# An attention and gated-MLP kernel rewritten around PSUM bank pairs and an order from a table

## The chip, the cores and the metric

The program runs on one core of one Trainium2 chip. A core has a matrix engine (TensorE, PE in the profile), a vector engine (VectorE, DVE), a scalar engine (ScalarE, ACT), GpSimd (POOL) and SyncE (SP), which here only issues transfers. Each engine works through its own instructions strictly in the order in which they stand, and waits for other engines on semaphores. Matmuls write to PSUM, a memory of eight banks of 512 float32 values for each of 128 partitions; ACT and DVE read PSUM, POOL can't. The metric is the time of one execution on the device, in microseconds (us); lower is better.

## The reference

The computation has two stages over 8 batches of 576 tokens. The first is a linear attention with 8 heads of width 64, the second a gated MLP over the 512 values that the heads give for each token.

```python
def phi(x):                                   # for q and for k
    proj = x @ w_phi                          # 64 -> 128 features
    proj = proj - max(abs(proj), over the features)
    return concat([exp(proj), exp(-proj)])    # 256 features
kv  = phi(k).T @ v                            # for each batch and head: 256 x 64
z   = sum of phi(k) over the tokens
x   = (phi(q) @ kv) / (phi(q) @ z + 1e-6)     # heads side by side: 576 x 512
h   = relu(x @ w_in)                          # 512 -> 1024
u, w = h[:, :512], h[:, 512:]
w   = (w - mean(w)) / sqrt(var(w) + 1e-6)     # over the 512 columns
w   = w_spatial @ w + b_spatial               # over the 576 tokens
out = (u * w) @ w_out                         # 512 -> 512
```

## The kernel before

Each batch's 576 tokens are four blocks of 128 ("main") and a tail of 64; the tails of two batches are joined to one block of 128. A unit of the first stage is one pair of heads of one batch (all four blocks), or the joined tail of two batches (all eight heads): 32 and 4 units. For a unit, q and k are brought to feature-major form, by PE transposes for the first batches and by transfers that transpose for the later ones; `by_token` (L229) then projects half a unit, four token-by-head blocks, into one PSUM bank with two matmuls of 256 columns, whose moving operand `wphi2` holds w_phi twice on a diagonal, for the two heads of a pair. For keys (`a_keys`, L236) DVE takes the maximum of the absolute values of that bank (L244) and ACT then takes exp(x) and exp(-x) of it (L247): each of the three instructions is 512 wide. The maximum of the keys is applied to v instead (`a_scale`, L264, multiplied on POOL at L272). Queries are projected twice. Once by token for the maximum (`a_queries`, L258); the maximum is split in a high and a low bfloat16 part (`mhl`), turned on PE (L293), and then subtracted inside the second, feature-major projection (`a_qfeat`, L296) by matmuls with the selection matrix `sel` (L308, 128 columns each). ACT takes both exponentials of it, again 512 wide (L321). `a_kv` (L326, matmuls L334 and L336) sums keys against values, `a_num` (L347, L354) multiplies query features with that sum, and `norm` (L341) divides on DVE (L344, L345).

The second stage, for one batch at a time, is `b_v` (L403, ReLU on ACT, statistics on DVE), `b_ln` (normalization on POOL, L420, with a root of four instructions, L413 to L416), `b_u` (L456), `b_s` (L477, gate on DVE, L480) and `b_o` (L500, copied by ACT, L502). It is PE work above all: matmuls of 512 columns.

Every PSUM tile of the kernel before is one bank, taken in turn from a pool of eight (`psum`, L57), and the framework places the semaphores. It also orders two engines that only read the same bank: the exponentials L247 wait for the maximum L244 of the same bank, though they don't use it.

The order of the work is made by loops. `step(i)` (L580) emits the parts of the units that are due (`ORDER`, L560, with lags of some units), and after each part `fill` (L568) emits tasks of the second stage from a queue, by a credit that counts PE's time. Loads are issued by POOL and SP from `io` (L622), some units ahead.

Of the kernel before, what the change touches and what calls it, by code (L numbers as in the profile page):

```python
# [12 lines left out]
AX = mybir.AxisListType  # L13


@with_exitstack
def kernel(
# [14 lines left out]

    nc = tc.nc

# [5 lines left out]
    P = 128  # L40
    KC = DM // P
    NP = H // 2
# [3 lines left out]
    G = B // 2  # L46
    POS = [0, 2, 1, 3]
    DA = D + 2

    cpool = ctx.enter_context(tc.tile_pool(name="const", bufs=1))  # L50
    ld = ctx.enter_context(tc.tile_pool(name="loads", bufs=2))
    a1 = ctx.enter_context(tc.tile_pool(name="stage_a", bufs=2))
    feat = ctx.enter_context(tc.tile_pool(name="feat", bufs=2))
    small = ctx.enter_context(tc.tile_pool(name="small", bufs=3))
    s2 = ctx.enter_context(tc.tile_pool(name="stage_b", bufs=2))

    psum = ctx.enter_context(tc.tile_pool(name="psum", bufs=8, space=bass.MemoryType.PSUM))  # L57


    def pin(start):  # L60
        return lambda *a, **kw: tc.keep_in_program_order(start(*a, **kw))

    def main_ap(t, b, h0=0, n=H):
        return bass.AP(tensor=t.tensor, offset=t.offset + (b * H + h0) * S * D,
                       ap=[[NB * D, P], [S * D, n], [1, NB * D]])
# [5 lines left out]
    st = {}  # L71
    gs = {}

    XB = 2

    def alloc(b):
        st[b] = dict(
            q=ld.tile([P, H, NB * D], BF16, tag="q_bf", name="q_bf", bufs=2),
            k=ld.tile([P, H, NB * D], BF16, tag="k_bf", name="k_bf", bufs=2),
            v=ld.tile([P, H * NB, D], FP32, tag="v_f", name="v_f"),  # L80
        )

    def alloc_tail(g):
        gs[g] = dict(
            q=ld.tile([P, H, D], BF16, tag="q_tl", name="q_tl", bufs=1),
            k=ld.tile([P, H, D], BF16, tag="k_tl", name="k_tl", bufs=1),
            v=ld.tile([P, H, D], FP32, tag="v_tl", name="v_tl", bufs=1),
        )

    def load(x, b, h0=0, n=H):  # L90
        if b not in st:
            alloc(b)
        pin(nc.gpsimd.dma_start)(out=st[b][x][:, h0:h0 + n], in_=main_ap(q if x == "q" else k, b, h0, n))

    def load_v(b, eng):
        pin(eng.dma_start)(out=st[b]["v"].rearrange("p (h c) d -> p h (c d)", h=H), in_=main_ap(v, b))

    def load_tail(x, g):
        if g not in gs:
            alloc_tail(g)  # L100
        t, eng = dict(q=(q, nc.gpsimd), k=(k, nc.gpsimd), v=(v, nc.sync))[x]
        for i in range(2):
            pin(eng.dma_start)(out=gs[g][x][i * TL:(i + 1) * TL], in_=tail_ap(t, 2 * g + i))

    def cross(b):
        d = st[b]
        for x in ("k", "q"):
            d[x + "T"] = ld.tile([P, 2 * H, P], BF16, tag=x + "T_b", name=x + "T_b", bufs=2)
            pin(nc.sync.dma_start_transpose)(out=d[x + "T"], in_=d[x].rearrange("p h x -> p (h x)"))


    wphi_f = cpool.tile([P, F], FP32)
    for i in range(2):
        nc.scalar.dma_start(out=wphi_f[i * D:(i + 1) * D, :], in_=w_phi)
    alloc(0)
    first = {}
    for x, t in (("k", k), ("q", q)):
        first[x] = s2.tile([P, 2, NB * D], FP32, tag="ob", name="first", bufs=4)
        pin(nc.sync.dma_start)(out=first[x], in_=main_ap(t, 0, 0, 2))
    ident = cpool.tile([P, P], BF16)  # L120
    make_identity(nc, ident)
    zero = cpool.tile([P, 1], BF16)
    pin(nc.vector.memset)(zero, 0.0)
    wphi2 = cpool.tile([P, 2 * F], BF16)
    pin(nc.vector.memset)(wphi2, 0.0)
    neghalf = cpool.tile([P, NB + 1], FP32)
    pin(nc.vector.memset)(neghalf, -0.5)

    w_spT = cpool.tile([P, NB + 2, S], BF16)
    pin(nc.vector.memset)(w_spT[:, NB:NB + 2, :], 0.0)  # L130

    NM = 3
    mhl, mT = [], []
    for i in range(NM):
        for tiles, name in ((mhl, "mhl"), (mT, "mT")):
            t = cpool.tile([P, P], BF16, name=f"{name}{i}")
            pin(nc.vector.memset)(t, 0.0)
            tiles.append(t)

    sel1 = cpool.tile([P, H], BF16)  # L140
    sel = cpool.tile([P, H, F], BF16)
    pin(nc.vector.tensor_tensor)(out=sel1, in0=ident[:, 0:H], in1=ident[:, H:2 * H], op=ALU.add)
    pin(nc.vector.tensor_scalar)(out=sel, in0=sel1.unsqueeze(2).to_broadcast([P, H, F]), scalar1=-1.0,
                                 scalar2=None, op0=ALU.mult)
    for x in ("k", "q"):
        pin(nc.vector.tensor_copy)(out=st[0][x][:, 0:2], in_=first[x])
    vst, vnt = [], []
    for i in range(2):
        t = cpool.tile([P, 2, 2, H, DA], BF16, name=f"vst{i}")
        pin(nc.scalar.copy)(out=t.rearrange("p b s h d -> p (b s h d)"), in_=zero.to_broadcast([P, 4 * H * DA]))  # L150
        vst.append(t)
        if i == 0:
            for y in range(2):
                r = slice(y * D, (y + 1) * D)
                pin(nc.scalar.copy)(out=wphi2[r, y * F:(y + 1) * F], in_=wphi_f[r, :])
        t = cpool.tile([P, 2, HALF], BF16, name=f"vnt{i}")
        for bl, row in ((0, TL), (1, 0)):
            pin(nc.scalar.copy)(out=t[:, bl, :], in_=ident[:, row:row + 1].to_broadcast([P, HALF]))
        vnt.append(t)
    load_v(0, nc.sync)  # L160
    for x in ("k", "q", "v"):
        load_tail(x, 0)
    load("k", 0, 2, 2)
    load("q", 0, 2, 2)
    load("k", 0, 4, 4)
    load("q", 0, 4, 4)

    w_in_bf = cpool.tile([P, KC, DFF], BF16)
    w_out_bf = cpool.tile([P, KC, DM], BF16)
    wsp = s2.tile([P, NB, T0], BF16, tag="vn", name="wsp", bufs=2)  # L170
    wspr = cpool.tile([P, NB, TL], BF16)
    wspt = ld.tile([TL, S], BF16, tag="kT_b", name="wspt", bufs=2)
    bsp_row = ld.tile([P, S], FP32, tag="qT_b", name="bsp_row", bufs=2)
    nc.sync.dma_start(out=bsp_row[TL:TL + 1, :], in_=moe_b_spatial)
    nc.sync.dma_start(out=bsp_row[0:1, :], in_=moe_b_spatial)

    rows = moe_w_spatial[0:T0, :].rearrange("(p c) s -> p c s", c=NB)
    cols = moe_w_in.rearrange("(kc p) f -> p kc f", p=P)

    def load_weight(out, in_):  # L180
        pin(nc.gpsimd.dma_start)(out=out, in_=in_)

    EARLY = 5
    XX = 9
    EK = 7
    def transpose_spatial(i):

        pt = psum.tile([P, S], BF16, tag="bank", name="pt")
        if i < NB:
            sc = POS[i]  # L190
            for tp, c in enumerate(POS):
                nc.tensor.transpose(out=pt[:, tp * P:(tp + 1) * P], in_=wsp[:, c, bass.ds(sc, P, step=NB)],
                                    identity=ident)
            nc.tensor.transpose(out=pt[:, T0:S], in_=wspt[:, bass.ds(sc, P, step=NB)],
                                identity=ident[:TL, :TL])
            nc.vector.tensor_copy(out=w_spT[:, i, :], in_=pt)
            return
        for bl in range(2):
            lo = bl * TL
            for tp, c in enumerate(POS):  # L200
                nc.tensor.transpose(out=pt[lo:lo + TL, tp * P:(tp + 1) * P], in_=wspr[:, c, :], identity=ident)
            nc.tensor.transpose(out=pt[lo:lo + TL, T0:S], in_=wspt[:, T0:S], identity=ident[:TL, :TL])
            nc.vector.tensor_copy(out=w_spT[lo:lo + TL, NB + bl, :], in_=pt[lo:lo + TL, :])
        for bl, row in ((0, TL), (1, 0)):
            r = slice(row, row + 1)
            pin(nc.scalar.copy)(
                out=w_spT[r, NB + bl, 0:T0].rearrange("o (a b p) -> o a b p", a=2, b=2),
                in_=bsp_row[r, 0:T0].rearrange("o (p b a) -> o a b p", a=2, b=2))
            pin(nc.scalar.copy)(out=w_spT[r, NB + bl, T0:S], in_=bsp_row[r, T0:S])


    def a_transpose(u):
        src = st[u["b"]] if u["pair"] else gs[u["g"]]
        if "kT" in src:
            for x in ("kT", "qT"):
                u[x] = src[x][:, 4 * u["pj"]:4 * u["pj"] + 4, :] if u["pair"] else src[x]
            return
# [18 lines left out]
    def a_keys(u):  # L236
# [4 lines left out]
        for half in range(2):  # L241
# [4 lines left out]
            for s, sc in ((0, 1.0), (1, -1.0)):  # L246
                nc.scalar.activation(out=u["kf"][:, s, hs, :], in_=pk, func=AF.Exp, bias=0.0, scale=sc)  # L247
# [436 lines left out]
```

## Time and profile before

| | |
|---|---|
| time, median of 3 runs | 289.59 us (288.79 to 296.42) |
| span of the profiled execution, first to last instruction | 286.4 us |
| median less that span | 3.2 us |
| granted TensorE clock | 1.000 |
| PE busy | 261.6 us (91%), 3070 matmuls |
| ACT busy | 229.3 us (80%), 517 instructions |
| DVE busy | 201.8 us (70%), 509 instructions |
| POOL busy | 182.2 us (64%), 320 instructions |
| first matmul | 4.29 us after the span's start |

The profile is of one execution. Its own time is known by its span of 286.4 us; what lies around the span is taken as the 3.2 us by which the median exceeds it. A busy time is the union of an engine's instructions from their starts to their ends. Instructions of one engine overlap in their ends (the next starts before the last has written all), so what an instruction costs in a row of its kind is the distance from its start to the next start, and is less than its mean duration; the timeline shows both.

### The profile page before, as it was taken

The page shows a single profiled execution, that of the slowest core. Times are in us where ns is not written, and L with a number is a line of the kernel's source. Part 1 is how long each engine was busy: PE and PEld are TensorE (multiplying, and loading weights), DVE is VectorE, ACT ScalarE, POOL GpSimd, SP SyncE. Part 2 cuts the span into 40 slices and gives each one's busy share as a digit, 9 for nine tenths or more (in the row PEclk, how much of TensorE's full clock was granted, in tenths as well). Part 3 has the DMA queues.
Part 4 walks back from the last instruction along what each step waited for, and adds up shares of the span by engine and source line. Part 5 has one row for each costly group of instructions (what it writes and reads, how often), then busy time and mean ns, then how long its engine had stood idle before and what let it go on. Part 6 is the DMA issues. An engine that isn't in the chain of part 4 may idle for free.

```text
span 286.4 us, 7965 instructions
## 1 busy us (share of the span) xinstructions
PE 261.6 (91%) x3070; PEld 178.6 (62%) x3070; DVE 201.8 (70%) x509; ACT 229.3 (80%) x517; POOL 182.2 (64%) x320
## 2 busy tenths in 40 slices
PE   1378889999999999999989999999999999999983
PEld 1157776777666776767557687666667676545441
DVE  4389997977958877598696887578688864354610
ACT  4949998899799988999998679799999746566033
POOL 8159998798336899479689954835969600058200
PEclk9999999999999999999999999999999999999999
DMA  6989999976568499999955994999111003500037
GB/s 185 203 171 120 206 219 223 163 203 71 79 147 186 102 187 155 173 245 196 130 94 102 225 191 87 264 287 255 32 22 32 7 2 122 211 3 0 0 90 242
DMA packets 81706, 40.31 MB, mean 141 GB/s; under 512 B 50242, under 2 KB 77058, under 8 KB 81668
## 3 DMA queue, kind: packets, MB, share of 16 engines
q1 hardware_dynamic: 54180, 28.32, 43.0%
q0 software_dynamic: 27328, 11.41, 35.5%
q8 instruction: 24, 0.39, 0.6%
q14 instruction: 14, 0.11, 0.2%
q10 hardware_dynamic: 160, 0.07, 0.1%
HBM read 32.85 MB, written 9.44 MB: 148 GB/s over the span
## 4 chain that ended last, share of the span: by engine, by line
PE 61%; ACT 14%; DVE 11%; DMA 9%; POOL 2%; issue 2%; ACTq 0%; SPq 0%; POOLq 0%; DVEq 0%
PE pv L403 10%; PE ps L477 8%; PE po L500 7%; PE pu L456 7%; PE ps L232 5%; ACT qf L321 5%; ACT kf L247 5%; PE pv L334 4%; DMA q_tl<-in_q_dram 4%; PE pn L354 4%; DMA out_dram<-ob 3%; PE pq L308 3%; PE pq L304 3%; DVE mk L244 3%; PE ps L478 2%; DVE mq L258 2%
## 5 line engine op out<-in xcount | busy, mean ns | idle before, releaser
L247 ACT ACTIVATE kf<-ps 128x512 bf16<-128x512 f32 x144 | 77.7, 692 | 5.6 <-DVE mk L244 5.4
L272 POOL TENSOR_TENSOR vs<-v_f,em 128x512 bf16<-128x512 f32 x64 | 65.6, 1049 | 23.6 <-ACT em L267 22.6
L321 ACT ACTIVATE qf<-pq 128x512 bf16<-128x512 f32 x128 | 68.2, 675 | 8.5 <-PE pq L308 8.5
L244 DVE TENSOR_REDUCE mk<-ps 128x4 f32<-128x512 f32 x72 | 46.1, 677 | 2.5 <-PE ps L232 2.0
L258 DVE TENSOR_REDUCE mq<-ps 128x4 f32<-128x512 f32 x62 | 39.9, 681 | 4.2 <-PE ps L232 3.4
L502 ACT COPY ob<-po 128x512 f32<-128x512 f32 (+1 forms) x37 | 21.6, 610 | 19.9 <-PE po L500 16.2
L406 DVE BATCH_NORM_STATS2 stats<-vr 128x6 f32<-128x512 bf16 (+1 forms) x37 | 24.8, 687 | 15.8 <-ACT vr L405 15.7
L477 PE MATMUL ps<-w_spT,vn 128*128 128x512 bf16 x128 | 32.8, 379 | 0.0
L456 PE MATMUL pu<-xT,w_in_bf 128*128 128x512 bf16 x128 | 31.6, 379 | 0.0
L403 PE MATMUL pv<-w_in_bf,xT 128*128 128x512 bf16 x128 | 31.2, 379 | 0.0
L480 DVE TENSOR_TENSOR uT<-ps,uT 128x512 bf16<-128x512 f32 x32 | 22.0, 689 | 12.7 <-PE ps L478 11.5
L500 PE MATMUL po<-w_out_bf,uT 128*128 128x512 bf16 x128 | 30.4, 379 | 0.0
L308 PE MATMUL pq<-mT,sel 128*128 128x128 bf16 x256 | 30.0, 219 | 0.0
L308 PEld LDWEIGHTS <-sel 128*128 128x128 bf16 x256 | 25.1, 98 | 3.9
L405 ACT ACTIVATE vr<-pv 128x512 bf16<-128x512 f32 (+1 forms) x37 | 23.3, 691 | 4.0 <-PE pv L403 3.9
L354 PEld LDWEIGHTS <-qf 128*128 128x128 bf16 x512 | 20.4, 97 | 8.2 <-issue 1.7
L345 DVE TENSOR_TENSOR x<-pn,rc 128x256 bf16<-128x256 f32 x64 | 25.0, 418 | 0.5
L420 POOL TENSOR_SCALAR vn<-vr,rs 128x512 bf16<-128x512 bf16 x32 | 24.3, 773 | 0.8
L334 PE MATMUL pv<-vs,kf 128*128 128x66 bf16 x512 | 24.5, 194 | 0.2 <-ACT kf L247 0.2
L354 PE MATMUL pn<-kv,qf 128*128 128x66 bf16 x512 | 22.3, 193 | 1.3 <-ACT qf L321 1.2
L334 PEld LDWEIGHTS <-kf 128*128 128x128 bf16 x512 | 21.7, 97 | 1.8 <-issue 0.9
L304 PE MATMUL pq<-qT_b,wphi 128*128 128x256 bf16 x96 | 22.4, 273 | 0.0
(120 smaller groups left out, 530.8 us busy)
## 6 DMA issues: line engine op xcount, KB each, us to landing
v_f<-in_v_dram SPq DMA_DIRECT2D x8, 1024.0 KB, 10.7
out_dram<-ob SPq DMA_DIRECT2D x32, 256.0 KB, 3.6
k_bf<-in_k_dram POOLq DMA_DIRECT2D x7, 512.0 KB, 7.0
q_bf<-in_q_dram POOLq DMA_DIRECT2D x7, 512.0 KB, 8.7
v_tl<-in_v_dram SPq DMA_DIRECT2D x8, 128.0 KB, 7.7
w_in_bf<-in_moe_w_in_dram POOLq DMA_DIRECT2D x2, 512.0 KB, 8.7
out_dram<-ob SPq DMA_DIRECT2D x8, 128.0 KB, 2.4
k_tl<-in_k_dram POOLq DMA_DIRECT2D x8, 64.0 KB, 6.8
```

The source lines that it names most:

```text
L244: nc.vector.tensor_reduce(out=u["mk"][:, hs], in_=pk, axis=AX.X, op=ALU.max, apply_absolute_value=True)
L247: nc.scalar.activation(out=u["kf"][:, s, hs, :], in_=pk, func=AF.Exp, bias=0.0, scale=sc)
L258: nc.vector.tensor_reduce(out=mq[:, 4 * half:4 * half + 4], in_=pq, axis=AX.X, op=ALU.max, apply_absolute_value=True)
L272: nc.gpsimd.tensor_tensor(out=vs[:, s, :, 0:D], in0=st[u["b"]]["v"][:, pj * H:(pj + 1) * H, :], in1=em[:, s, :].unsqueeze(2).to_broadcast( ...
L308: nc.tensor.matmul(out=pq[:, 2 * par + x, :], lhsT=sel[:, j, :], rhs=m, start=False, stop=(x == 1))
L321: nc.scalar.activation(out=qf[:, s], in_=pq, func=AF.Exp, bias=0.0, scale=sc)
L334: nc.tensor.matmul(out=pv[:, hh, s, :], lhsT=u["kf"][:, s, 4 * hh + c, :], rhs=u["vs"][:, s, 4 * hh + c, :], start=(c == 0), stop=False)
L354: nc.tensor.matmul(out=pn[:, pos, :], lhsT=u["qf"][hh][:, s, pos, :], rhs=d["kv"][:, 2 * u["pj"] + hh, s, :], start=(s == 0), stop=(s == 1))
L403: nc.tensor.matmul(out=pv[r], lhsT=lhs(kc), rhs=w_in_bf[:, kc, HALF:DFF], start=(kc == 0), stop=(kc == KC - 1))
L456: nc.tensor.matmul(out=pu, lhsT=w_in_bf[:, kc, dc * P:(dc + 1) * P], rhs=d["xT"][:, kc, :], start=(kc == 0), stop=(kc == KC - 1))
L477: nc.tensor.matmul(out=ps, lhsT=d["vn"][:, sp, cs], rhs=w_spT[:, sp, 0:T0], start=(sp == 0), stop=False)
L500: nc.tensor.matmul(out=po[r], lhsT=lhs(dc), rhs=w_out_bf[:, dc, :], start=(dc == 0), stop=(dc == KC - 1))
```

## The change

The kernel is written anew; the computation, the engines that take most of its parts and the number of cores stay. What differs:

- **Query units.** A unit of queries is two token blocks by four heads (32 units), no longer four blocks by two heads. Key units stay a pair of heads by four blocks.
- **Half-row projections.** `wphi` holds w_phi twice, one copy in partitions 0 to 63 and one in 64 to 127. A projection contracts 64 partitions: the even head's matmul uses the upper half of the array's rows and the odd head's the lower half, each writing another bank. By token that is eight matmuls of 128 columns for a unit; feature-major it is two of 512 columns, and eight with half of `sel`.
- **Operations over bank pairs.** All of PSUM is one tile `ps` of eight banks; `pair(i, j)` is an access pattern over banks i and j, with the step j - i. The maxima, the exponentials and the division of a unit each read such a pair in one instruction of 1024 (the division 512) elements.
- **Order and places from a table.** `ORDER` is a text of 1418 words. Each names a part of the work with its indices, the numbers of the buffers or banks it takes, and the engine where there is a choice. The words are emitted from the first to the last, with no scheduler and no pools behind them. 56 of its 144 bank pairs are neighbours, 25 are six or seven banks apart.
- **Smaller moves.** 34 of the 72 ReLUs, 13 of the 36 output copies and 11 of the 32 copies of the key sums go to DVE; the root is one instruction on DVE and one on POOL, for two blocks; transposes by transfer are of half a batch; the tails of batches 0 and 1 are joined as the others are; 18 matmuls on the identity stand at the start.

```diff
-    psum = ctx.enter_context(tc.tile_pool(name="psum", bufs=8, space=bass.MemoryType.PSUM))
+    psum = ctx.enter_context(tc.tile_pool(name="ps", bufs=1, space=bass.MemoryType.PSUM))
+    ps = psum.tile([P, 8, 512], FP32, name="banks")
...
+    def bank(i):
+        return ps[:, i, :]
+
+    def pair(i, j):
+        return ps[:, bass.ds(i, 2, step=j - i), :]
...
-    def by_token(xT, half):
-        ps = psum.tile([P, 4, F], FP32, tag="bank", name="ps")
-        for x in range(2):
-            nc.tensor.matmul(out=ps[:, 2 * x:2 * x + 2, :], lhsT=xT[:, 2 * half + x, :], rhs=wphi2,
-                             start=True, stop=True)
-        return ps
+    def by_token(xT, banks):
+        for n in range(HH):
+            for y in range(2):
+                nc.tensor.matmul(out=bank(banks[y])[:, n * F:(n + 1) * F], lhsT=xT[halves[y], n, :],
+                                 rhs=wphi[halves[y], :], start=True, stop=True)
+        return pair(*banks)
+
+    def maxima(out_, pp):
+        nc.vector.tensor_reduce(out=out_, in_=pp.rearrange("p y (n f) -> p y n f", f=F), axis=AX.X, op=ALU.max,
+                                apply_absolute_value=True)
+
+    def key_exp(pp, kf, s):
+        nc.scalar.activation(out=kf[:, s].rearrange("p y n f -> p y (n f)"), in_=pp, func=AF.Exp, bias=0.0,
+                             scale=(1.0, -1.0)[s])
...
+    def features(u, xT, banks):
+        m = at["mT", u]
+        for y in range(2):
+            nc.tensor.matmul(out=bank(banks[y]).rearrange("p (n t) -> p n t", n=HH), lhsT=wphi[halves[y], :],
+                             rhs=xT[halves[y]], start=True, stop=False)
+        for n in range(HH):
+            for y in range(2):
+                nc.tensor.matmul(out=bank(banks[y])[:, n * P:(n + 1) * P], lhsT=sel[halves[y], n, :],
+                                 rhs=m[halves[y], :], start=False, stop=(n == HH - 1))
+        at["pq", u] = pair(*banks)
+
+    def query_exp(u, s):
+        nc.scalar.activation(out=at["qf", u][:, s].rearrange("p y n t -> p y (n t)"), in_=at["pq", u], func=AF.Exp,
+                             bias=0.0, scale=(1.0, -1.0)[s])
+
+    def sums(banks):
+        return pair(*banks)[:, :, 0:HH * DA].rearrange("p y (n d) -> p y n d", d=DA)
...
+    def qx(e, b, cc, hg, place=None):
+        u = (b, cc, hg)
+        if place is not None:
+            take("x", (b, cc), place)
+        nc.vector.tensor_tensor(out=at["x", (b, cc)][:, :, hg * HH:(hg + 1) * HH, :], in0=at["pn", u][:, :, :, 0:D],
+                                in1=at["rc", u].to_broadcast([P, 2, HH, D]), op=ALU.mult)
...
+    with tc.manual_schedule():
+        for word in ORDER.split():
+            word, _, e = word.partition("@")
+            name, _, places = word.partition(":")
+            name, *args = name.split(".")
+            places = [int(x) for x in places.split(",")] if places else []
+            ops[name](e, *map(int, args), *places)
```

One line of the table, as an example: keys are projected by `kp` (batch, pair of heads, two banks), their maxima are `km`, their exponentials `ke`; queries are `qp`, `qm`, `qf`, `qe`; `qn` multiplies with the key sums, `qr` and `qx` divide.

```
qr.0.0.0:1 qx.0.0.0:1 lq.2:2 qn.0.0.1:2,5 lv.1.1:1@S xq.1.1:0 ckt.1:0@P km.1.0:1 kp.1.1:4,6 lqt.1:1@S qr.0.0.1:2
qx.0.0.1 xk.2.0:2 tx.0.1:2 qe.0.1.1.0:3 km.1.1:0 qe.0.1.1.1 tx.0.0:5 ke.1.0.0:4 qn.0.1.1:1,3 vst.0.1.0@P txc.0.0:0@V
```

More of the change, by code (lines that the diff above doesn't have):

```diff
@@ L105, in cross @@
[L105 to L119, printed above, removed]
@@ L140 @@
[L140 to L159, printed above, removed]
@@ L174 @@
[L174 to L188, printed above, removed]
+    rows = [slice(0, TL), slice(TL, 2 * TL)]
@@ new lines, in zsp, with warm, lkf @@
+    @op
+    def zsp(e):
+        ENG[e].memset(w_spT[:, NB:NB + 2, :], 0.0)
+    @op
+    def warm(e, n, place):
+        for i in range(n):
+            nc.tensor.matmul(out=bank(place)[:, 0:F], lhsT=ident, rhs=ident, start=True, stop=True)
+    @op
+    def lkf(e, j, *places):
+        if j == 0:
+            take("ld", ("k", 0), places[0])
+        take("ob", ("k", j), places[-1])
+        ENG[e].dma_start(out=at["ob", ("k", j)].rearrange("p (h x) -> p h x", h=2), in_=main_ap(k, 0, 2 * j, 2))
@@ new lines, in ckt, with cqt, lvt, lin @@
+    @op
+    def ckt(e, g, place):
+        copy(e, take("tl", ("k", g), place), at["tf", ("k", g)])
+    @op
+    def cqt(e, g, place):
+        copy(e, take("tl", ("q", g), place), at["tf", ("q", g)])
+    @op
+    def lvt(e, g, place):
+        t = take("vt", g, place)
+        for i in range(2):
+            ENG[e].dma_start(out=t[rows[i]], in_=tail_ap(v, 2 * g + i))
+    @op
+    def lin(e, i):
+        cs = slice(HALF, DFF) if i == 0 else slice(0, HALF)
+        nc.gpsimd.dma_start(out=w_in[:, :, cs], in_=moe_w_in.rearrange("(kc p) f -> p kc f", p=P)[:, :, cs])
@@ new lines, in xk, with xq, turn @@
+    @op
+    def xk(e, b, h2, place):
+        cross("k", b, h2, place)
+    @op
+    def xq(e, b, h2, place):
+        cross("q", b, h2, place)
+    def turn(x, b, h2, i, place):
+        pt = bank_bf(place).rearrange("p (n t) -> p n t", t=P)
+        src = at["ld", (x, b)][:, h2 * HH:(h2 + 1) * HH]
+        for j in range(4):
+            nc.tensor.transpose(out=pt[:, j, :], in_=src[:, 2 * i + j // 2, (j % 2) * P:(j % 2 + 1) * P],
+                                identity=ident)
+        at["pT", (x, b, h2, i)] = pt[:, 0:4, :]
@@ new lines, in turn_tail, with tkt, tqt, tktc @@
+    def turn_tail(x, g, place):
+        pt = bank_bf(place).rearrange("p (n t) -> p n t", t=P)
+        for j in range(HH):
+            nc.tensor.transpose(out=pt[:, j, :], in_=at["tl", (x, g)][:, 2 * j:2 * j + 2, :], identity=ident)
+        at["pT", (x, g)] = pt[:, 0:HH, :]
+    @op
+    def tkt(e, g, place):
+        turn_tail("k", g, place)
+    @op
+    def tqt(e, g, place):
+        turn_tail("q", g, place)
+    @op
+    def tktc(e, g, place):
+        copy(e, take("tT", ("k", g), place), at["pT", ("k", g)])
@@ new lines, in qe, with qn @@
+    def qe(e, b, cc, hg, s, place=None):
+        if place is not None:
+            take("qf", (b, cc, hg), place)
+        query_exp((b, cc, hg), s)
+    @op
+    def qn(e, b, cc, hg, p0, p1):
+        u = (b, cc, hg)
+        f = at["qf", u]
+        at["pn", u] = sums((p0, p1))
+        for y in range(2):
+            for n in range(HH):
+                for s in range(2):
+                    nc.tensor.matmul(out=at["pn", u][:, y, n, :], lhsT=f[:, s, y, n, :],
+                                     rhs=at["kv", b][:, hg * HH + n, s, :], start=(s == 0), stop=(s == 1))
@@ new lines, in qnt, with qrt @@
+    @op
+    def qnt(e, g, p0, p1):
+        at["pn", g] = sums((p0, p1))
+        for y in range(2):
+            for n in range(HH):
+                for s in range(2):
+                    for bl in range(2):
+                        r = rows[bl]
+                        nc.tensor.matmul(out=at["pn", g][r, y, n, :], lhsT=at["qf", g][:, s, y, n, r],
+                                         rhs=at["kv", 2 * g + bl][:, 2 * n + y, s, :], start=(s == 0), stop=(s == 1))
+    @op
+    def qrt(e, g, place):
+        nc.vector.reciprocal(out=take("rc", g, place), in_=at["pn", g][:, :, :, D:D + 1])
@@ new lines, in um, with ur @@
+    @op
+    def um(e, b, dc, place):
+        for kc in range(KC):
+            nc.tensor.matmul(out=bank(place).rearrange("p (c t) -> p c t", c=NB),
+                             lhsT=w_in[:, kc, dc * P:(dc + 1) * P], rhs=at["xT", b][:, :, kc, :], start=(kc == 0),
+                             stop=(kc == KC - 1))
+        at["pu", (b, dc)] = bank(place)
+    @op
+    def ur(e, b, dc, place=None):
+        if place is not None:
+            take("uT", b, place)
+        relu(e, at["uT", b][:, dc, :], at["pu", (b, dc)])
@@ new lines, in om, with oc, od @@
+    @op
+    def om(e, b, c, place):
+        for dc in range(KC):
+            nc.tensor.matmul(out=bank(place), lhsT=at["uT", b][:, dc, c * P:(c + 1) * P], rhs=w_out[:, dc, :],
+                             start=(dc == 0), stop=(dc == KC - 1))
+        at["po", (b, c)] = bank(place)
+    @op
+    def oc(e, b, c, place):
+        copy(e, take("ob", (b, c), place), at["po", (b, c)])
+    @op
+    def od(e, b, c):
+        dst = bass.AP(tensor=out.tensor, offset=out.offset + (b * S + c) * DM, ap=[[NB * DM, P], [1, DM]])
+        ENG[e].dma_start(out=dst, in_=at["ob", (b, c)])
@@ L648 @@
[L648 to L653 removed]
+            for c in range(NB):
+                nc.tensor.matmul(out=pt[:, dc, :], lhsT=at["vn", 2 * g + bl][:, c, cs], rhs=w_spT[:, c, T0:S],
+                                 start=(c == 0), stop=False)
+            nc.tensor.matmul(out=pt[:, dc, :], lhsT=at["vnt", g][:, bl, cs], rhs=w_spT[:, NB + bl, T0:S],
+                             start=False, stop=True)
@@ new lines, in smt, with sgt, omt, oct @@
+        at["psp", g, bl] = pt
+    @op
+    def sgt(e, g, bl):
+        u = at["uTt", g][:, :, rows[bl]]
+        nc.vector.tensor_tensor(out=u, in0=at["psp", g, bl], in1=u, op=ALU.mult)
+    @op
+    def omt(e, g, place):
+        for dc in range(KC):
+            nc.tensor.matmul(out=bank(place), lhsT=at["uTt", g][:, dc, :], rhs=w_out[:, dc, :], start=(dc == 0),
+                             stop=(dc == KC - 1))
+        at["po", g] = bank(place)
+    @op
+    def oct(e, g, place):
+        copy(e, take("ob", g, place), at["po", g])
```

1029 lines of the change are left out of this document (569 added, 460 removed).

## The prediction

> **What bounds the kernel now.** I read the totals first, then the chain that ended last, then timelines of single engines for what one instruction costs in a row.
>
> ```profile
> span 286.4 us, 7965 instructions
> ...
> PE 261.6 (91%) x3070; PEld 178.6 (62%) x3070; DVE 201.8 (70%) x509; ACT 229.3 (80%) x517; POOL 182.2 (64%) x320
> ...
> PE 61%; ACT 14%; DVE 11%; DMA 9%; POOL 2%; issue 2%; ACTq 0%; SPq 0%; POOLq 0%; DVEq 0%
> ```
>
> PE is busiest and holds 61% of the chain. The chain in order of time (start, us, what) gives PE's price of a matmul:
>
> ```profile
> 169.74 0.45 PE pt L225 x8
> ...
> 206.90 0.50 PE pn L354 x16
> ...
> 209.83 0.44 PE ps L232 x4
> 210.27 0.86 PE pv L403 x4
> ```
>
> So 216 ns for 512 columns (L403), 109 for 256 (L232), 56 for 128 (L225), 31 for 66 (L354): PE is fed without gaps. The kernel before sums to 247.9 us by these prices, in a span that begins PE's work at 4.29 us; most of PE's idle time lies in the first 47 us (it is busy 8.1 of the first 20), where the chain runs through DVE and ACT. Hence after 47 us PE sets the time.
>
> Two timelines of PE (start, us, instructions) show what the new shapes meet:
>
> ```profile
> 131.13 0.72 PE L382 MATMUL pn<-kv,qf_t 128*64 128x66 bf16 x32
> 131.79 0.39 PE L456 MATMUL pu<-xT,w_in_bf 128*128 128x512 bf16 x1
> ...
> 86.02 0.38 PE L403 MATMUL pv<-w_in_bf,xTt 128*64 128x512 bf16 x1
> 86.34 0.67 PE L354 MATMUL pn<-kv,qf 128*128 128x66 bf16 x16
> ```
>
> 32 matmuls on alternating halves of the array's columns take 0.66 us, 18 ns each where a whole-array one costs 31: two halves run side by side. And from the half-array matmul at 86.02 to the whole-array one is 0.32 us where 0.216 is the price: a change of array shape costs about 96 ns. The other changes of shape give 94 to 121.
>
> For DVE and ACT the same view:
>
> ```profile
> 38.75 1.27 DVE L258 TENSOR_REDUCE mq<-ps 128x4 f32<-128x512 f32 x2
> 39.94 0.23 DVE L344 RECIPROCAL rc<-pn 128x4 f32<-128x4 f32 x2
> ...
> 58.04 2.10 ACT L247 ACTIVATE kf<-ps 128x512 bf16<-128x512 f32 x4
> 59.95 0.37 ACT L267 ACTIVATE em<-mk 128x8 f32<-128x8 f32 x2
> ```
>
> A 512-wide maximum takes 0.598 us in a row, an exponential 0.478. With the 256-wide rows (L345 0.331, L470 0.264) the fixed part is 64 ns on DVE, 50 on ACT; 1024 wide is then 1.132 and 0.905 us.
>
> The last view is the list of waits (us in total, times, longest):
>
> ```profile
> ACT kf L247 <- DVE mk L244: 5.4, 4, 3.3
> ```
>
> The exponential uses nothing of the maximum; both only read the same bank. So the program already puts readers of one bank one behind the other.
>
> **The change part by part, engines first.** *By token*: 288 matmuls of 109 ns (31.4 us) become 576 of 56, two at a time: 16.1. *Feature-major*: 128 of 109 and 320 of 56 (31.9) become 72 of 216 and 288 of 56, two at a time: 15.8. Fewer transposes and joined tails give another 5 us: 247.9 becomes 211.6. Against it stand changes of shape: counted in the built order, 117 in place of 34, at 96 ns 11.2 in place of 3.3. PE: 251.2 to 223 us, a gain of 28, if row halves pair as column halves do. No row here shows row halves; the ends are 0 and 32 us of pairing, and I take all of it, by the column rows above. The Trainium skill ("TensorE: Matmul & The Clock Gate", Measured speedup vs the span model) gives four row tiles 3.07 times the speed, not 4; by that share the paired matmuls would cost some 10 us more, an estimate.
>
> *ACT*: 288 exponentials (137.7 us) become 144 (130.3); 34 ReLUs go to DVE (16). *DVE*: 144 maxima (86.1) become 72 (81.5); it gains 34 ReLUs (20) and 13 output copies (8). In the built order ACT sums to 178 us, DVE 193, POOL 171: all under PE.
>
> By stages of a sixteenth of PE's work, the busiest engine of each sums to 124.3 us for the first seven stages (there DVE, ACT or POOL) and 122.6 for the other nine (PE). With 4.3 at the start and 4 at the end (last copy 0.7, last store 3.2) that would be a span of 255.
>
> **The wait that the change adds.** It takes this away. A read of `pair(0, 7)` is one access pattern over PSUM, and in the built order its waits cover every bank from 0 to 7. Of 1478 waits between compute engines, 280 join two instructions that share neither bank nor buffer, only banks that lie between. The third key maximum (banks 0 and 7) waits for an exponential of banks 5 and 6; the transposes into bank 4 that follow wait for that maximum. Behind such a transpose stands all of PE's queue; behind a maximum or an exponential held up so stand DVE's divisions and ACT's copies, for which PE waits in turn. So readers of a wide pair shut PE, ACT and DVE out of the banks between.
>
> What that costs I add up on one bank, 3, since of 213 changes of engine among those that hold it, 209 are enforced by waits. In the first seven stages:
>
> - PE writing it: 268 matmuls, 13.0 us.
> - 42 maxima at 1.132: 47.5.
> - 38 key exponentials at 0.905: 34.4; 36 query exponentials: 32.5.
> - 16 divisions with their reciprocals: 10.8; other copies: 6.4.
> - 147 changes of engine: 25.1. One costs what an instruction lasts beyond its price in a row (PE 163 ns, ACT 150, DVE 83, durations less distances) and the gap to the waiting one (medians of the waits: 34 to 38 ns, 55 to PE).
>
> Together 169.6 us, of which 82.9 are readers that don't touch bank 3; with their own banks alone it would be 78.0. From there PE's remaining work follows in its order: 120.2 us and 25 changes of shape, 122.6. The span is then at least 4.3 + 169.6 + 122.6 + 4 = 300.5 us.
>
> To that come what the chain waits for outside bank 3. Stage by stage the busiest bank is not always 3 (the chain passes to another at a wide read that covers both): 34.5, 28.3, 25.7, 31.1, 26.4, 19.3 and 16.2, together 181.5: 12 more. At the start, loads issued on POOL's queue landed 12 to 15 us after issue in the trace, and the first stage needs them: I add 6 (ends 0 and 12). In stages 8 to 11 the busiest bank comes within 0.2 to 4 us of PE's 13.8, so some waits show: 6 (ends 0 and 16). Sum: 324.5. With the 3.2 us that the median lies over the span of before, **328 us**.
>
> **Rivals.**
>
> 1. *Row halves don't pair.* Nothing in the profile shows them pairing. PE's unpaired cost falls as 9 us in the last nine stages, 3 on bank 3, and up to 10 more where PE meets the bank waits: 340 to 350. Chance 0.12.
> 2. *The reads of different banks run side by side after all*, faster than before. Mechanism: the table was ordered so that instructions the widened waits join rarely meet. It would give the 255 of the engine sums, with up to 16 us of idle as PE had in the first 47 us: a time of 258 to 274. It decides if the bank-3 chain is mostly covered, under 110 us. Against it: the chain's 169.6 is work, not coincidence; it can't be covered by other work on the bank. The Trainium skill ("PSUM — Partial Sum Buffer", Specifications) says that ACT and DVE can read PSUM in parallel at full speed without a bank collision; by that rule the chip would allow this case, but the semaphores of the program don't, and they decide. Chance 0.04.
> 3. *The waits bind half*: PE writes ahead into banks outside the boxes and the sum of 169.6 overlaps with PE's later work by 12 us or more: 284 to 295, no change. Chance 0.04.
>
> The forecast itself has 0.80: chiefly 301 to 352. The low end is the sum without additions (300.5 and 3.2), less 3 that PE may run ahead where its stages join the bank's; the high end takes the upper ends of the three additions (12, 12, 16: 340.5) or the first rival, and 3.2 and some idle more: 352. The range 301 to 352 leaves out the second and third rival and the top of the first. A difference under 2% (5.8 us) can't be told from none here. Faster 0.04, same 0.04, slower 0.92.
>
> **What would show each step.** In the profile of the changed kernel: PE's busy share falls well under 91% and its idle time is ended by DVE maxima and ACT exponentials on matmuls of other banks; maxima (L522) near 1.13 us and exponentials near 0.91 in a row, where they stand in a row; ACT's exponentials wait for DVE's maxima and divisions; the seventh sixteenth of PE's work ends near 200 us and the rest is dense. By-token matmuls (L517) start 28 ns apart, or 56 under the first rival. I am wrong if PE stays over 85% busy from 50 us on, or if time is lost to transfers: the cross transposes and loads on SP's queue, each behind waits, are not in my sum.

## The result and the profile after

The changed kernel takes 449.59 us (median of 4 runs, 445.38 to 454.95), the kernel before 290.24 beside it: a ratio of 1.540 (95% interval 1.531 to 1.549). The direction was forecast with 0.92; the size was not. 328 us was predicted, 301 to 352 the range, and the measured time lies 98 us beyond its upper end. The ratio leaves out runs over 1.5% slower than the fastest of the same kernel (it compares 445.38 and 446.88 us with 288.79 to 290.89), while medians and ranges are of all runs.

The totals of the changed kernel, two rows of its 40 slices (the clock that PE was granted, in tenths, and the busy share of the DMA engines) and the chain that ended last:

```profile
span 443.6 us, 7949 instructions
...
PE 290.5 (65%) x3184; PEld 171.9 (39%) x3184; DVE 221.6 (50%) x411; ACT 195.2 (44%) x314; POOL 216.0 (49%) x280
...
PEclk9556655666966766666677869999999999999999
DMA  8999965150980633936044748174233115012245
...
PE 30%; ACT 8%; DVE 8%; issue 2%; POOL 1%; DVEq 0%; ACTq 0%; POOLq 0%
```

No engine is over 65% busy. For the first 24 slices (265 us) the granted clock lies mostly between 0.5 and 0.7, which it never did before. The shares of the chain add up to 49%: the page follows it only part of the way, so it can't carry the explanation here.

In the list of waits (us in total, times, longest) two waits of POOL for data lead, 66.5 and 62.1 us. PE, ACT and DVE have no entry over 24.0 us, but many like these:

```profile
ACT kf L526 <- DVE mk L522: 20.4, 6, 7.2
...
ACT qf L642 <- DVE x L702: 11.3, 5, 4.0
PE banks L517 <- ACT kf L526: 11.2, 6, 3.4
```

The first stood at 5.4 us before. The second is an exponential that waits for a division, the third a projection that waits for an exponential: pairs that exchange no data.

What such a wait is can be seen in the timelines of PE, ACT and DVE in one stretch (start, us, instruction, and in brackets the idle time before it and what ended it):

```profile
154.78 1.09 PE L689 MATMUL banks<-kv,qf 128*128 128x66 bf16 x16
156.84 0.37 PE L633 MATMUL banks<-T,wphi 64*128 64x512 bf16 x1 [0.97 <-DVE mq L522]
158.14 0.37 PE L633 MATMUL banks<-T,wphi 64*128 64x512 bf16 x1 [0.93 <-DVE rc L695]
158.14 0.59 PE L637 MATMUL banks<-mT,sel 64*128 64x128 bf16 x8
160.97 0.61 PE L517 MATMUL banks<-wphi,T 64*128 64x128 bf16 x8 [2.24 <-ACT qf L642]
...
156.82 1.02 ACT L526 ACTIVATE kf<-banks 128x1024 bf16<-128x1024 f32 x1 [3.75 <-DVE mq L522]
158.12 1.02 ACT L526 ACTIVATE kf<-banks 128x1024 bf16<-128x1024 f32 x1 [0.28 <-DVE rc L695]
159.90 1.02 ACT L642 ACTIVATE qf<-banks 128x1024 bf16<-128x1024 f32 x1 [0.76 <-DVE x L702]
...
155.56 1.23 DVE L522 TENSOR_REDUCE mq<-banks 128x8 f32<-128x1024 f32 x1 [3.54 <-PE banks L689]
...
157.88 0.21 DVE L695 RECIPROCAL rc<-banks 128x8 f32<-128x8 f32 x1 [0.96 <-ACT kf L526]
...
159.17 0.69 DVE L702 TENSOR_TENSOR x<-banks,rc 128x512 bf16<-128x512 f32 x1 [0.47 <-ACT kf L526]
```

With the bank numbers from the table, this is one relay: maximum of banks 0 and 5 (155.56), exponential of 3 and 4 (156.82), reciprocal of 1 and 7 (157.88), the other exponential of 3 and 4 (158.12), division of 1 and 7 (159.17), exponential of 0 and 5 (159.90), projection into 2 (160.97). Each starts when the one before it ends; no two neighbours of this list share a bank or a buffer; and PE, which has work for other banks in its queue, stands behind the one matmul that waits.

I joined all instructions of the trace with the waits of the built program. Idle time that ended with an instruction which shares neither bank nor buffer with the waiting one, only banks that lie between, comes to 165.7 us on ACT (69 waits), 141.8 on DVE (73) and 85.6 on PE (60). Idle time that a user of the same bank ended comes to 51.2, 56.1 and 43.0.

Where the time went, by sixteenths of PE's work (its instructions in their order, at the prices of the prediction; the table gives the time at which a share of that work was done, in us of each profiled execution):

| kernel | 2/16 | 4/16 | 7/16 | 12/16 | 16/16 |
|---|---|---|---|---|---|
| before | 56.2 | 89.7 | 137.5 | 218.9 | 282.0 |
| after | 113.4 | 197.6 | 290.3 | 386.1 | 439.4 |
| e4: every pair two apart | 97.2 | 164.7 | 237.6 | 363.5 | 417.2 |
| e2: every pair neighbours | 80.4 | 124.4 | 176.2 | 258.6 | 312.3 |
| e3: e2, multiply-add | 77.7 | 118.3 | 167.4 | 249.4 | 302.4 |
| e9: e3, read bank by bank | 77.8 | 119.3 | 168.0 | 249.1 | 302.9 |
| e1: after, read bank by bank | 78.8 | 122.3 | 171.8 | 247.9 | 300.4 |
| e5: e1, multiply-add | 77.7 | 115.6 | 163.8 | 233.8 | 286.3 |
| e6: e5, 48 transposes on PE, new banks | 65.0 | 108.3 | 159.9 | 242.1 | 296.3 |
| e8: e6 with e5's banks | 69.2 | 108.5 | 157.2 | 227.3 | 281.4 |
| e10: e5, 16 transposes on PE | 79.4 | 118.0 | 168.2 | 237.6 | 291.3 |

The changed kernel loses 153 us on the one before in its first seven sixteenths, and gets nothing of it back; the last four take 13.3 us each, as priced. (In the traces of some runs a few dozen of the 3184 matmul records are missing, so a row can be off by 1%.)

### The profile page after: what moved, and what is told of

It reads as the page before. It is cut to its first block, busy times and chain, and to the rows that moved or that the text cites. A ratio compares the mean times of both kernels' runs of the same rounds, so it can differ in the third digit from the quotient of the medians.

```text
span 443.6 us, 7949 instructions
## 1 busy us (share of the span) xinstructions
PE 290.5 (65%) x3184; PEld 171.9 (39%) x3184; DVE 221.6 (50%) x411; ACT 195.2 (44%) x314; POOL 216.0 (49%) x280
## 5 line engine op out<-in xcount | busy, mean ns | idle before, releaser
L642 ACT ACTIVATE qf<-banks 128x1024 bf16<-128x1024 f32 x72 | 71.9, 1024 | 79.8 <-PE banks L880 11.9
L575 POOL TENSOR_TENSOR vs<-v,em 128x512 bf16<-128x512 f32 x62 | 64.1, 1041 | 87.5 <-ACT em L532 66.5
L526 ACT ACTIVATE kf<-banks 128x1024 bf16<-128x1024 f32 x64 | 65.1, 1027 | 64.6 <-DVE mk L522 20.4
L522 DVE TENSOR_REDUCE mq<-banks 128x8 f32<-128x1024 f32 x36 | 43.9, 1220 | 47.7 <-PE banks L608 9.6
L809 POOL TENSOR_SCALAR vn<-vr,mv,rs 128x512 bf16<-128x512 bf16 x30 | 62.1, 2073 | 1.1
L522 DVE TENSOR_REDUCE mk<-banks 128x8 f32<-128x1024 f32 x36 | 43.8, 1220 | 29.3 <-PE banks L608 9.4
L798 PE MATMUL banks<-w_in,xT 128*128 128x512 bf16 x128 | 40.0, 446 | 13.6 <-DVE x L702 4.2
L806 POOL TENSOR_TENSOR rs<-mv,neghalf 128x2 f32<-128x2 f32 (+1 forms) x20 | 13.7, 684 | 66.1 <-DVE mv L803 62.1
L895 PE MATMUL banks<-w_spT,vn 128*128 128x512 bf16 x128 | 36.3, 410 | 7.9 <-ACT kf L526 4.3
L880 PE MATMUL banks<-xT,w_in 128*128 128x512 bf16 x128 | 35.8, 415 | 2.4 <-ACT ob L253 1.5
L909 PE MATMUL banks<-w_out,uT 128*128 128x512 bf16 x128 | 33.8, 401 | 3.4 <-DVE x L702 2.0
L798 PEld LDWEIGHTS <-xT 128*128 128x128 bf16 x128 | 12.7, 107 | 29.2 <-issue 19.6
```

Of the source, the lines that this page charges most:

```text
L522: nc.vector.tensor_reduce(out=out_, in_=pp.rearrange("p y (n f) -> p y n f", f=F), axis=AX.X, op=ALU.max, apply_absolute_value=True)
L526: nc.scalar.activation(out=kf[:, s].rearrange("p y n f -> p y (n f)"), in_=pp, func=AF.Exp, bias=0.0, scale=(1.0, -1.0)[s])
L575: ENG[e].tensor_tensor(out=at["vs", (b, j)][:, s, :, 0:D], in0=at["v", (b, j // 2)][:, (j % 2) * n:(j % 2 + 1) * n, :], in1=at["em", (b, j ...
L642: nc.scalar.activation(out=at["qf", u][:, s].rearrange("p y n t -> p y (n t)"), in_=at["pq", u], func=AF.Exp, bias=0.0, scale=(1.0, -1.0)[s])
L798: nc.tensor.matmul(out=bank(place), lhsT=lhs[:, kc, :], rhs=w_in[:, kc, HALF:DFF], start=(kc == 0), stop=(kc == KC - 1))
L809: ENG[e].tensor_scalar(out=out_, in0=in_, scalar1=mv, scalar2=rs, op0=ALU.subtract, op1=ALU.mult)
```

## The experiments

**e1: the same pairs, read bank by bank.** Every maximum, exponential and division of a pair becomes two instructions, one for each bank. The table, the bank numbers and the order stay. The theory of the prediction ("waits") stands against the rival that order, clock or transfers make the time.

```diff
-        nc.scalar.activation(out=at["qf", u][:, s].rearrange("p y n t -> p y (n t)"), in_=at["pq", u], func=AF.Exp,
-                             bias=0.0, scale=(1.0, -1.0)[s])
+        for y in range(2):
+            nc.scalar.activation(out=at["qf", u][:, s, y].rearrange("p n t -> p (n t)"), in_=at["pq", u][:, y],
+                                 func=AF.Exp, bias=0.0, scale=(1.0, -1.0)[s])
```

> The changed kernel's table, order, buffers and banks, but every read of a bank pair is made as two instructions of one bank each (maxima, exponentials, reciprocals, divisions). No wait then joins instructions over a bank that only lies between. Theory 'waits' (the widened waits of wide pairs make the engines take turns): time 270 to 295, the engine sums of the stages (262 with the normalization on POOL at the 2.07 us that it took) plus about 12 for twice the instructions; granted clock back to 1.0. Theory 'order' (the table itself puts the work in an order that starves PE, and the half clock that follows does the rest): over 400, clock near 0.8. Theory 'POOL' (the normalization that takes 2.07 us in place of 0.77 holds the second stage up): 380 or more, with POOL's idle time gone.

Measured: 307.04 us (303.40 to 308.38), 1.053 times the kernel before (1.042 to 1.064). 143 us are gone with nothing but the shape of 288 reads. The totals, clock and DMA rows of this run:

```profile
PE 246.6 (81%) x3151; PEld 151.0 (50%) x3184; DVE 224.8 (74%) x555; ACT 199.5 (66%) x458; POOL 215.9 (71%) x280
...
PEclk9955697956979997999999999999999899999999
DMA  6999999999998998799999967255225101031256
```

PE's busy time falls by 44 us though its matmuls are the same, since the clock is back for most of the run. So the wide reads are the main cause; but the time is not at the 270 to 295 expected, and the table shows the rest of the loss in the first four sixteenths (122.3 against 89.7).

**e2: neighbours only.** The reads stay 1024 wide. Only bank numbers in the table change (some of its words, before and after), so that all 144 pairs are neighbours and no bank lies between.

```diff
-kp.0.0:1,2   tk.0.0.1:3   kp.0.1:5,6   kp.0.2:0,7   kp.0.3:1,3
+kp.0.0:2,3   tk.0.0.1:5   kp.0.1:0,1   kp.0.2:4,5   kp.0.3:6,7
```

> The changed kernel with nothing but other numbers of banks in the table: all 144 pairs are neighbours, so no bank lies between; order, buffers, instructions and their widths as they were. Theory 'waits': 262 to 285 (engine sums of the stages 262, start and end 8, some idle time), a little under the split version since each wide read keeps its one fixed part. Theory 'order': as the changed kernel, over 400. Theory 'POOL': 380 or more.

Measured: 316.94 us (314.71 to 320.15), ratio 1.089 (1.079 to 1.099). That is above the 262 to 285 expected, but it confirms the cause from another side: wide operations as such cost little, the banks between cost 133 us. It is 10 us slower than e1, and I first took that for a price of wide operations; e9 shows that it isn't.

**e3: e2 with another normalization.** The profile after has a price that the prediction left out. On POOL:

```profile
L809 POOL TENSOR_SCALAR vn<-vr,mv,rs 128x512 bf16<-128x512 bf16 x30 | 62.1, 2073 | 1.1
```

Before, the same block was normalized by a multiply and an add (times in ns: least, median, most):

```profile
L420 POOL TENSOR_SCALAR vn<-vr,rs x32: 766/772/778, 57.8 to 266.2; 128x512 bf16<-128x512 bf16 x32
```

e3 goes back to these two operations, with two more small instructions for minus mean times root:

```diff
-        ENG[e].tensor_scalar(out=out_, in0=in_, scalar1=mv, scalar2=rs, op0=ALU.subtract, op1=ALU.mult)
+        ENG[e].tensor_scalar(out=out_, in0=in_, scalar1=rs[:, 0:1], scalar2=rs[:, 1:2], op0=ALU.mult, op1=ALU.add)
```

> As the version with neighbouring pairs, and the normalization on POOL is a multiplication and an addition as in the kernel before (two more small POOL instructions for two blocks), in place of a subtraction and a multiplication. The instruction falls from 2.07 us to 0.77 if the operations are the reason. Theory 'waits': 5 to 15 us under the neighbouring pairs, since POOL was the busiest engine of three or four stages. Theory 'POOL': 40 us or more under it. If the 2.07 us come from something else (two engines at one port), no change.

Measured: 308.34 us (307.75 to 310.80), ratio 1.064 (1.054 to 1.074), and

```profile
L811 POOL TENSOR_SCALAR vn<-vr,rs x30: 758/771/778, 92.2 to 282.5; 128x512 bf16<-128x512 bf16 x30
```

On POOL, subtract and multiply take 2.7 times as long as multiply and add on the same block; 8.6 us of the time hang on it. (The two per-partition operands also moved into one tile, which wasn't tried alone. The two blocks that DVE normalizes show no difference: 404 to 407 ns in the changed kernel, 405 in e5.)

**e4: one bank between.** Again only bank numbers change: every pair is two apart. 266 waits still join instructions that share neither bank nor buffer (280 in the changed kernel), but each wide read now shuts out one bank, not up to six.

```diff
-kp.0.0:1,2   kp.0.1:5,6   kp.0.2:0,7   kp.0.3:1,3
+kp.0.0:4,6   kp.0.1:5,7   kp.0.2:1,3   kp.0.3:0,2
```

> A half dose: the changed kernel with other numbers of banks, every pair two apart, so that each wide read shuts out just one bank that it does not use (the table had 1.9 on average, up to six). Theory 'waits': between the neighbouring pairs and the changed kernel, 340 to 390. Theory 'order' or 'POOL': as the changed kernel, over 420.

Measured: 421.55 us (417.28 to 423.12), ratio 1.449 (1.437 to 1.462), above what I expected.

```profile
PE 290.4 (69%) x3151; PEld 173.2 (41%) x3184; DVE 219.2 (52%) x411; ACT 195.3 (46%) x314; POOL 216.4 (51%) x280
```

PE's busy time is that of the changed kernel (290.5). This run tells most about the prediction. Its way of reckoning, the work that holds one bank added up, gives for e4 a worst bank (number 2) of 119 us in the first seven sixteenths. That is less than the busiest engine needs there (124.3), so by that reckoning e4 should run at the engines' pace, some 260 us. It ended its seventh sixteenth at 237.6. So the load of one bank doesn't set the length of the chain here. (The 340 to 390 on record for this run was a guess at a weaker dose, and missed as well.)

**e5: e1 and e3 together.** One-bank reads, the table's own bank numbers, multiply and add.

> Every pair read by two one-bank instructions, as in the first run, and the normalization on GpSimd as multiply and add, as in the third. Both theories: the gain of the third over the second (8.6 us) comes on top of the first, 307 - 9 = 298 us (294 to 303), the operation at L821 at 0.77 us instead of 2.07. If the gain of the multiply and add lay only in freeing wide reads earlier, less than 3 us, above 304.

Measured: 291.21 us (288.59 to 297.57), ratio 0.989 (0.976 to 1.001): no difference from the kernel before, whose fastest run beside it took 288.98. The time lies below the 294 to 303 expected: the gain on e1 is 16 us, more than the 9 of e3. 14 of the 16 are there by the twelfth sixteenth (247.9 against 233.8), where POOL has the normalizations beside the first stage's products; that this is the reason is argued, not shown.

**e6 and e7: fewer transposing transfers at the start.** In e1, PE waited early for tiles transposed by transfer:

```profile
PE banks L517 <- DMA T<-ld: 19.3, 3, 9.6
```

In e6 q of batch 0 and k and q of batch 1 are transposed by PE, in e7 without q of batch 1 (48 and 32 matmuls of 128 columns; the 24 in the text below miscounts them). Places for the new transposes came from giving all banks anew, as neighbours where possible.

```diff
-xq.0.0:1   xq.0.1:3
+tq.0.0.0:6   tqc.0.0.0:1@V   tq.0.0.1:4   tqc.0.0.1@A   tq.0.1.0:5   tqc.0.1.0:3@V   tq.0.1.1:4   tqc.0.1.1@A
```

> The kernel with one-bank reads and multiply-add, in which q of batch 0 and k and q of batch 1 are transposed by TensorE (24 transposes, twelve copies out) and no longer by six transfers; bank numbers are given anew. 'The start waits for transposing transfers' (PE idle for T: 1.6, 9.6 and 8.1 us in the first run, one transposing transfer holding the queue of SyncE for 7.5 us): the first four sixteenths end 12 to 25 us earlier than without it (122 us in the first run), time 275 to 288, below the kernel before. 'The start is late for another reason' (half clock, the order, the pairs): the same as without it within 5 us, 293 to 303, and the idle time turns up on another wait.

> As the one before, but q of batch 1 stays with the transfers: only the two waits that cost 9.6 and 8.1 us in the first run (batch 0's q and batch 1's k) lose their transfers. 'The start waits for transposing transfers': most of the gain, 278 to 292. 'Another reason': 293 to 303.

Measured: e6 302.98 us (298.12 to 304.09), ratio 1.022 (1.004 to 1.040); e7 304.55 (302.04 to 309.88), 1.033 (1.017 to 1.049). Their fastest runs are 3 and 5% above the 288.98 of the kernel before. By the time alone "another reason" wins. The table says otherwise: after two sixteenths e6 is 12.7 us ahead of e5, as the transfer theory wants (after four it is 7.3 ahead of e5 and 14.0 ahead of e1, with 12 to 25 on record), and after twelve it is 8.3 us behind. Two things had changed at once, transposes and bank numbers.

**e8: e6 with e5's bank numbers.** Every bank keeps the number that it has in e5; only the 12 new transposes (of four matmuls each) get banks.

> As e6 (q of batch 0, k and q of batch 1 transposed by TensorE, one-bank reads, multiply-add), but every pair and bank that e5 has keeps its bank number; only the 12 new transposes get banks of their own. e6 was 13 us ahead of e5 after two sixteenths (65.0 against 77.7 us) and lost 18 us between the sixth and the twelfth (16 to 18 us each against 14). 'The new bank numbers of e6 cost it that' (which bank is taken when it has only just been read): the start of e6 and the pace of e5, 275 to 285 us. 'The transposes by TensorE cost it later' (the order was fitted to the late start): 293 to 303 as e6.

Measured: 284.58 us (284.08 to 287.22), ratio 0.982 (0.975 to 0.989).

```profile
PE 249.7 (87%) x3232; PEld 154.9 (54%) x3232; DVE 227.0 (80%) x561; ACT 201.9 (71%) x464; POOL 175.1 (61%) x320
...
PEclk9955679799989999997999999999999999999999
```

It keeps most of e6's start (69.2 and 108.5 at two and four sixteenths) and runs on at e5's pace. So both theories had a part: the transfers delayed the start, and e6's bank numbers cost what that had won. e8 is the one kernel here whose interval lies below the kernel before; at 1.8% it is still under the 2% that I call a difference.

**e9: e3's bank numbers, read bank by bank.** Against e3 only the width of the reads differs, against e5 only the bank numbers.

> e3's bank numbers (pairs of neighbours) with e5's one-bank reads, so against e3 (308) only the width of the reads differs, against e5 (291) only the bank numbers. 'Wide operations cost the 17 us between e3 and e5': 288 to 295. 'The bank numbers cost them': 302 to 310.

Measured: 310.34 us (308.85 to 312.58), ratio 1.072 (1.064 to 1.080). e3 with 1024-wide reads took 308.34. On neighbours, then, the width of an operation is worth nothing in time, and the 19 us to e5 are the bank numbers (the two ran at different times; the fastest run of the kernel before took 288.08 us beside e9 and 288.98 beside e5): idle time of PE that a reader of the very bank ended is 23.4 us in e9 and 6.3 in e5. I take it that the table's own numbers put more time between a bank's reader and its next writer; that time wasn't measured.

**e10: only q of batch 0 on PE.** As e8, but two transfers are replaced (16 matmuls), not six.

> As e8, but only q of batch 0 is transposed by TensorE (two transfers fewer, not six). Of the two waits of 9.6 and 8.1 us the first is gone. 'Bank numbers': 280 to 289. 'Transposes by TensorE cost it later': 290 to 300.

Measured: 296.55 us (292.68 to 297.35), ratio 1.017 (1.008 to 1.026): not faster, though the first wait is gone. The timelines of SyncE and of PE:

```profile
21.09 13.27 SPq L452 DMA_TRANSPOSE T<-ld  x2
34.46 11.27 SPq L367 DMA_DIRECT2D tf<-in_k_dram  x2
...
50.94 1.04 PE L518 MATMUL banks<-wphi,T 64*128 64x128 bf16 x16 [11.33 <-DMA T<-ld]
```

The next transfers in SyncE's queue start earlier and are then held there for 13.3 and 11.3 us; in place of e1's two long waits of 9.6 and 8.1 us stand one of 11.3, one of 2.8 and one of 1.5, and the first sixteenth ends at 52.6 us (48.6 in e5). The time falls in the range of the second theory, but neither named this mechanism, and it covers only part of the loss: after two sixteenths e10 is 1.7 us behind e5, at the end 5.0, and what cost it the rest is open. Here two transfers fewer didn't help, and six fewer (e8) did.

## Why the prediction was right in direction and wrong in size

*Engine prices: right.* Four matmuls of 512 columns still follow each other at 0.86 us at the end, where nothing waits:

```profile
400.91 1.03 PE L798 MATMUL banks<-w_in,xT 128*128 128x512 bf16 x4
401.77 1.03 PE L955 MATMUL banks<-w_out,uTt 128*128 128x512 bf16 x4
```

In a row, 1024-wide exponentials start 0.90 to 0.92 us apart (0.905 predicted) and maxima 1.13 (1.132). e5, which has the changed kernel's order without its wide reads, does the stages from the fourth to the twelfth sixteenth in 14.8 us each, against 16.2 before.

*Row halves pair: right, and the first rival is out.* Two matmuls of a half-row projection start 4 ns apart and the next two 57 ns after the first, so 28 ns each as predicted. e5 shows it where nothing waits, with eight matmuls of 128 columns in 0.23 us:

```profile
109.92 0.43 PE L639 MATMUL banks<-mT,sel 64*128 64x128 bf16 x8
110.15 0.81 PE L517 MATMUL banks<-wphi,T 64*128 64x128 bf16 x16
```

The 10 us that the Trainium skill's 3.07-fold speed for four row tiles would have added aren't seen in these pairs.

*The widened waits decide: right.* e1 and e2 take them away in two ways that share nothing else, and 143 and 133 of the 159 us between the two kernels go. The second and third rival are out.

*The sum on one bank: this step failed.* The prediction put the first seven sixteenths at 4.3 us of start, 169.6 on bank 3, 12 for other banks and 6 for loads: 192, "near 200". They took 290.3. I followed the chain of the trace back through the program's waits from the end of the seventh sixteenth to 7.8 us: 189 stretches of one engine each, 140 of them begun by a wait for an instruction that shares neither bank nor buffer, 46 by one for the same bank, 3 by one for a buffer.

| part of the chain, to 290.3 us | predicted | measured |
|---|---|---|
| DVE and ACT, with the changes of engine | 156.6 | 151.4 |
| PE | 13.0 | 121.2 |
| POOL | not counted | 9.9 |

The chain passes over some 42 maxima and 79 exponentials, where 42 and 74 were counted, so the readers were right. That the sums agree to 5 us is in part luck: the predicted one holds the changes from and to PE too. The term of 13.0 us, "PE writing it", was wrong: I counted only matmuls that write bank 3 and let all other work of PE run beside the chain. 104.3 of PE's 121.2 us are stretches that begin on a matmul that does not write bank 3. It can't run beside the chain, since PE's queue is strict: a matmul for bank 2, 4 or 5 that waits for a wide read holds up all that stand behind it, and the next wide read waits in its turn for what PE writes inside its own range. So the three engines take turns (the relay above), and the chain takes in work of all three wherever it lies. e4 shows the same without an overloaded bank.

*The clock: left out.* 92.6 of the 121.2 us of PE on the chain ran at a granted clock of half speed, where a 512-column matmul takes 426 ns, not 216: at most about 46 us (half of 92.6, an estimate) of the 98 by which these stages miss. The Trainium skill ("TensorE: Matmul & The Clock Gate", HAM oscillation) warns of PE pauses above some 3.4 us that halve the clock, and in the section after it ("A second HAM failure mode: psum-queue depth-cycling") of small pauses between bursts when matmuls cycle through banks. The trace is nearer the second case: of PE's pauses only 5 are longer than 3.4 us and 58 lie between 1 and 3.4, and the clock went down 19 times for 171 us in all. In the stretch shown above, pauses of at most 2.24 us left PE busy for 5.4 of 13 us, at a mean clock of 0.63. How much of the 449 us the clock alone makes wasn't tried on the chip: a kernel that keeps PE busy in the pauses needs a bank that no wide read shuts out.

*Stages 8 to 16: half right.* Predicted were 122.6 for PE, 6 for waits and 4 for the end; they took 153.3. Sixteenths 8 to 12 took 95.8 us with PE busy for 72.8 of them, so 23 us of idle where 6 were allowed for; that this is the same error on a smaller scale is likely, but wasn't followed up. The last four are as priced.

*What the prediction named and didn't count.* The transposing transfers and loads on SyncE's queue stood in its last sentence as a way to be wrong. They cost nothing visible while the waits ruled, and some 7 to 13 us at the start once these were gone (e8, e6). The slow normalization is hidden in the changed kernel (POOL is on its chain for 9.9 us) and worth 9 to 16 us without the waits. The pieces that were "faster" in the change (pairing, wide operations) add up to e5, which is as fast as the kernel before, not to a gain: its first four sixteenths take 26 us longer, and the rest 22 less.

## What to carry to other kernels

An operand that steps over PSUM banks is guarded as the whole range from its first to its last bank, and a single bank between is enough for nearly the full loss (1.45 against 1.54): pair neighbours, or read bank by bank, which here cost no time that shows (310.3 against 308.3 us). When such waits couple engines with strict queues, don't add up the load of one bank; follow the chain from engine to engine and let everything count that stands in the queue ahead of the waiting instruction, with the clock in mind (here it was halved for 171 of 444 us). Which bank is written next matters even without any width (19 us between two numberings of one order), and a wait taken away shows only if what stands next in the same queue isn't late too (e10).

## What the runs showed of the hardware that I had not expected

- On POOL, subtract-and-multiply with two per-partition operands on 128 x 512 bfloat16 takes 2073 ns, multiply-and-add 758 to 778; on DVE both take 404 to 407.
- The granted clock halves for stretches of 3.4 us and their multiples although PE seldom pauses for that long: PE's busy time was 290.5 us for work that takes 242.1 in e5 (where 33 of the matmul records are missing).
- Two 512-wide reads of PSUM on ACT or DVE cost the kernel no time that shows against one of 1024 (310.3 and 308.3 us), though e1's ACT is busy for 199.5 us and e2's for 191.7.
- One transposing transfer held SyncE's queue for up to 7.5 us in e1 and e5, at a time when the DMA engines were full (digits of 9); in the changed kernel, where for the most part they weren't, the median was 1.3.
